# Softcapped attention ahead of two feed-forward layers: first keys loaded in two pieces, exps over three chunks, and the last keys' exps added to the sums by accumulating transfers

## The chip, the core and the metric

The kernel runs on one core of a Trainium2 chip. The core has a matmul engine (PE, with its weight loads shown apart as PEld), a vector engine (DVE), an activation engine (ACT), a general engine (POOL) and a queue engine that issues transfers (SP); POOL and ACT can issue transfers as well. Sixteen DMA engines move the data. Each engine works through its own list of instructions in order, and semaphores tie the lists together. The metric is the time of one execution in microseconds (us); lower is better.

## The reference

Attention over 2 batches and 12 heads with 448 positions and a head width of 64, then two feed-forward layers of 896 tokens, width 768 and inner width 2048. All in fp32.

```python
scores = scale * np.matmul(q, k.transpose(0, 1, 3, 2))
scores = cap * np.tanh(scores / cap)
attn = np.exp(scores - np.max(scores, axis=-1, keepdims=True))
attn = attn / (np.sum(attn, axis=-1, keepdims=True) + 1e-09)
x = np.matmul(attn, v)                    # heads side by side: 896 x 768
h = x @ w_in
x = (np.maximum(h, 0.0) + alpha * np.minimum(h, 0.0)) @ w_out
r = np.maximum(x @ w_in2, 0.0)
return (r * r) @ w_out2
```

## The kernel before

**Stages.** The attention takes about the first 97 us of the execution, the first feed-forward layer runs from there, the second after it. The feed-forward stages follow an order that a planner in the kernel worked out beforehand. The change doesn't touch the planner. The attention is written out by hand in `fast_attention`: six steps u = 0 to 5, and in each step four heads (two head pairs g = 0, 1, and two heads e = 0, 1 in a pair). The rows of PE, ACT and DVE stand in the order of the code. POOL and SP are ordered by the compiler from the same code.

**One step.** The 448 keys of a pair are cut in three full chunks of 128 keys and a rest of 64. So a step has seven chunks: 0 to 2 are the full chunks of pair 0, 3 to 5 those of pair 1, and chunk 6 holds both rests, pair 0 in partitions 0 to 63 and pair 1 in partitions 64 to 127. For every chunk PE multiplies keys with queries (`product`, lines 800 and 804) into one of three PSUM tiles `ps`, which are taken in turn; ACT takes the tanh of it into an SBUF tile `E` (line 819), which frees the PSUM tile, and later the exp in place (line 824). DVE adds up the exps over the chunks (`presum`): parts 1 and 2 add the chunks 0 to 2 to `s` of pair 0, parts 4 and 5 add the chunks 3 to 5 to `s` of pair 1 (line 840), and parts 6 and 7 add the two halves of chunk 6 to the two `s` (line 844, half of the partitions each). A step later PE multiplies the exps with the values (`values`, `last_values`, lines 852 and 862) and reduces the two `s` over the partitions with a matrix of ones (`sums`, line 871), which takes a `ps` tile too.

**A step's tail.** `evacuate` copies the sums (line 877, tile `rows`) and the two output tiles (line 883, `xu`) out of PSUM. Small transfers spread `rows` over partitions (line 880, tile `r`), `invert` takes 1/r on DVE and sends it on (lines 889 to 895, tile `rb`), and `normalise` multiplies `xu` with `rb` and splits the product in two parts for the next layer (lines 921 to 924). So step u runs the products, tanhs and exps of u, the values and sums of u - 1, the evacuation and the inverses of u - 2 and the normalisation of u - 3. Beside them `advance` prepares weights of the first feed-forward layer on DVE (lines 333 to 339, 938, 940).

**The end of the attention.** After step 5 PE runs three blocks of the first layer (`up_now`) among the rest: `up_now(0)`, the values and sums of step 5, `up_now(1)`, then `spread_last` (line 913), which needs the reciprocal of the last sums (line 903 on DVE, after line 902 on ACT), then `up_now(2)`.

**The start.** In `start`, SP issues the first keys and the first queries, one transfer each, while PE runs eight matmuls that only warm it up (line 766). Then PE multiplies the first 128 keys (line 771), and ACT starts on them.

Of the kernel before, what the change touches and what calls it, by code (L numbers as in the profile page):

```python
# [17 lines left out]
P = 128  # L18
# [6 lines left out]
FULL = 3  # L25
# [273 lines left out]
class Net:  # L299
# [443 lines left out]
    def start(self, ctx):  # L743
# [9 lines left out]

        first = self.raw[:, 1].bitcast(F32).rearrange("p n f -> p (n f)")
        k, q = (first[:, n * S:n * S + S] for n in range(2))
        nc.sync.dma_start(k, self.kT[:, 0])
        nc.sync.dma_start(q, self.qT[:, 0])
        self.kq = {0: (k, q)}
        self.ones = const.tile([P, P // 4], F32, name="ones")
        nc.gpsimd.memset(self.ones, 1.0)  # L760
# [46 lines left out]
    def tanh(self, u, *chunks):  # L807
        nc, S = self.nc, self.S
        es = self.es.setdefault(u, [])
        for n in chunks:  # L810
            if n % 2 == 0:
                shape = [P, min(2, 2 * FULL + 1 - n), 2, S]
                es.append(self.ap.tile(shape, F32, tag=f"E{shape[1]}", name="E", bufs=5 if shape[1] == 2 else 2))
            if u == n == 0:
                for e in range(2):
                    nc.scalar.activation(es[0][:, 0, e], self.outs[e], AF.Tanh, scale=self.scale_t)
                continue
            ps = self.early[n] if u == 0 and n in self.early else self.product(u, n)
            nc.scalar.activation(es[-1][:, n % 2], ps, AF.Tanh, scale=self.scale_t)  # L819

    def exp(self, u, m):

# [1 line left out]
        self.nc.scalar.activation(x, x, AF.Exp, scale=self.cap_t)  # L824

    def chunk(self, u, n):
        return self.es[u][n // 2][:, n % 2]

    def presum(self, u, *parts):

        nc, D, S = self.nc, self.D, self.S
        for part in parts:
            if part < 2 * FULL:
                g, c = divmod(part, FULL)
                if c == 0:
                    continue
                if c == 1:
                    self.ss[u, g] = self.ap.tile([P, 2, S], F32, tag="s", name="s", bufs=3)
                s = self.ss[u, g]
                nc.vector.tensor_add(s, self.chunk(u, part - 1) if c == 1 else s, self.chunk(u, part))  # L840
            else:
                rows = slice((part - 2 * FULL) * D, (part - 2 * FULL) * D + D)
                s = self.ss[u, part - 2 * FULL]
                nc.vector.tensor_add(s[rows], s[rows], self.chunk(u, 2 * FULL)[rows])

    def values(self, u, g):

# [94 lines left out]
    def fast_attention(self):  # L942
# [17 lines left out]
        for u in range(n):  # L960
            if u > 1:
                self.evacuate(u - 2)
            self.tanh(u, 0, 1, 2)
            self.exp(u, 0)
            if u:
                self.values(u - 1, 0)
                self.presum(u - 1, 4, 5, 6, 7)
                if u + 1 < n:
                    for g in range(2):
                        self.load_kq(2 * u + 2 + g)  # L970
            if u > 2:
                self.normalise(u - 3)
            self.tanh(u, 3, 4)
            self.exp(u, 1)
            self.presum(u, 1)
            if u > 1:
                self.invert(u - 2)
            if u:
                self.values(u - 1, 1)
                for m, steps in beside[u]:  # L980
                    self.advance(m, steps)
            self.tanh(u, 5, 6)
            if u < AHEAD - 1:
                self.fetch(u + 1)
            self.exp(u, 2)
            self.exp(u, 3)
            self.presum(u, 2)
            if u:
                self.last_values(u - 1)
                self.sums(u - 1)  # L990
                if u + 1 < n:
                    self.load_v(u + 1)
# [182 lines left out]
```

## Time and profile before

| | |
|---|---|
| runs of the kernel before | 521.12, 523.66, 524.09 us; median 523.66 |
| the profiled execution's own time | 522.88 us |
| its span in the profile | 520.8 us |
| busy in the span | PE 503.9 us (97%), DVE 469.2 (90%), ACT 395.0 (76%), POOL 36.9 (7%) |
| shares of the chain that ended last | PE 62%, DVE 15%, ACT 12%, DMA 5% |

How to read the rows further down: a row of the timeline is start, length, engine, line, operation, tile written `<-` tiles read, shape; `x2` merges two instructions in a row, and a bracket at the end says how long the engine had been idle before and for whom it waited. A row of the windows gives the stretch, its length and the busy time of each engine in it with the count of instructions, then the granted clock of PE, the mean busy share of the DMA engines and GB/s. The profiled execution's time of 522.88 us is its span plus 2.08 us around it.

### The profile page before, as it was taken

Reading aid. Unit: us, or ns where it says so; the run is one execution under the profiler, and the core shown is the slowest. Engines: PE = TensorE matmul, PEld = TensorE weight load, DVE = VectorE, ACT = ScalarE, POOL = GpSimd, SP = SyncE. Lnnn points to the kernel's source line nnn. Section 1 sums busy time; section 2 is a strip of 40 time slices with the busy share of each in tenths; the row PEclk is TensorE's granted clock in tenths of the full one; section 3 lists DMA queues with packets and bytes.
Section 4 is the critical chain, followed back from the end, with each engine's and each line's share of the span. In section 5 each row is a group of like instructions: output and inputs, shape, how many; then the busy total and the mean of one; then the engine's idle time right before and its main releaser. Section 6 shows DMA issues by size and latency. Waiting matters only on the chain.

```text
span 520.8 us, 6996 instructions
## 1 busy us (share of the span) xinstructions
PE 503.9 (97%) x2532; PEld 418.7 (80%) x2532; DVE 469.2 (90%) x698; ACT 395.0 (76%) x547; POOL 36.9 (7%) x51
## 2 busy tenths in 40 slices
PE   7899899999999999999999988999999999999996
PEld 2233234899999999999999977888989999999995
DVE  1689999899989999999979998899999999999961
ACT  6999994467687889755999947999677889946450
POOL 1000000000000000061500000100000002410000
PEclk9999999999999999999999999899999999999999
DMA  5744623156767565176835406566342229750011
GB/s 174 291 167 143 204 73 99 35 182 194 243 233 235 172 241 198 62 132 119 152 124 151 123 0 197 146 202 186 96 148 90 106 76 270 144 95 35 37 72 59
DMA packets 25195, 74.29 MB, mean 143 GB/s; under 512 B 4544, under 2 KB 15168, under 8 KB 25152
## 3 DMA queue, kind: packets, MB, share of 16 engines
q1 hardware_dynamic: 19392, 63.72, 37.4%
q0 software_dynamic: 5616, 10.03, 10.8%
q8 instruction: 22, 0.36, 0.3%
q14 instruction: 21, 0.17, 0.1%
q10 hardware_dynamic: 144, 0.00, 0.0%
HBM read 60.89 MB, written 2.79 MB: 122 GB/s over the span
## 4 chain that ended last, share of the span: by engine, by line
PE 62%; DVE 15%; ACT 12%; DMA 5%; issue 4%; SPq 1%; POOL 0%; DVEq 0%; ACTq 0%; POOLq 0%
PE hm L352 43%; PE out L352 14%; ACT raw L387 3%; DVE wl L434 2%; DMA r<-rows 2%; ACT wh L432 2%; ACT w L393 2%; DVE s L840 2%; DMA raw<-in_w 1%; ACT E L824 1%; ACT x L432 1%; ACT E L819 1%; PE ps L800 1%; DVE x L434 1%; PE out L852 1%
## 5 line engine op out<-in xcount | busy, mean ns | idle before, releaser
L352 PE MATMUL hm<-x,wh 128*128 128x448 f32 x916 | 258.1, 363 | 0.5 <-ACT g L509 0.4
L352 PEld LDWEIGHTS hm<-x,wh 128*128 128x128 f32 x916 | 171.7, 188 | 13.3 <-ACT g L509 1.6
L352 PE MATMUL hm<-x,wl 128*128 128x448 f32 x458 | 165.9, 362 | 0.0
L352 PEld LDWEIGHTS hm<-x,wl 128*128 128x128 f32 x458 | 86.0, 188 | 5.8
L352 PE MATMUL out<-x,wh 128*128 128x448 f32 x296 | 83.4, 362 | 0.2
L432 ACT CAST wh<-w 128x768 fp32r<-128x768 f32 x67 | 53.7, 805 | 22.0 <-PE hm L352 8.7
L432 ACT CAST x<-g 128x448 fp32r<-128x448 f32 x93 | 51.3, 571 | 22.3 <-DVE g L407 22.2
L387 ACT ACTIVATE raw<-raw 128x768 f16<-128x768 f32 x32 | 63.1, 1973 | 3.5 <-DVE raw L395 3.5
L434 DVE TENSOR_TENSOR wl<-w,wh 128x768 fp32r<-128x768 f32 x67 | 60.4, 902 | 1.1 <-ACT wh L432 0.9
L352 PEld LDWEIGHTS out<-x,wh 128*128 128x128 f32 x296 | 55.3, 187 | 4.6 <-ACT g L509 0.9
L434 DVE TENSOR_TENSOR x<-g,x 128x448 fp32r<-128x448 f32 x93 | 57.1, 616 | 0.6 <-ACT x L432 0.5
L352 PE MATMUL out<-x,wl 128*128 128x448 f32 x148 | 53.6, 362 | 0.0
L393 ACT ACTIVATE w<-raw 128x768 f32<-128x768 f32 x44 | 40.8, 931 | 11.4 <-DMA raw<-in_w 6.8
L391 DVE SCALAR_TENSOR_TENSOR w<-w,raw 128x768 int32<-128x768 int32 x44 | 41.8, 953 | 8.1 <-ACT raw L387 6.1
L819 ACT ACTIVATE E<-ps,scale_t 128x896 f32<-128x896 f32 x41 | 40.2, 1074 | 1.8 <-PE ps L800 1.8
L824 ACT ACTIVATE E<-E,cap_t 128x1792 f32<-128x1792 f32 (+1 forms) x24 | 38.9, 1667 | 0.0
L800 PE MATMUL ps<-q,k 64*128 64x448 f32 x132 | 30.4, 570 | 5.1 <-DVE rows L877 2.1
L407 DVE TENSOR_TENSOR g<-g,g 128x448 f32<-128x448 f32 x55 | 33.6, 616 | 1.1 <-ACT g L647 0.9
L352 PE MATMUL hm<-cx,wh 128*128 128x448 f32 x98 | 28.7, 375 | 3.1 <-ACT early L509 2.6
L432 ACT CAST wh<-cw 128x768 fp32r<-128x768 f32 x26 | 21.9, 844 | 12.7 <-DVE cw L407 6.5
L800 PEld LDWEIGHTS ps<-q,k 64*128 64x128 f32 x132 | 11.0, 185 | 24.5 <-ACT E L819 12.0
L852 PE MATMUL out<-E,v 128*64 128x448 f32 x144 | 29.5, 547 | 0.0
(141 smaller groups left out, 670.6 us busy)
## 6 DMA issues: line engine op xcount, KB each, us to landing
raw<-in_w SPq DMA_DIRECT2D x64, 768.0 KB, 4.2
x<-g POOLq DMA_DIRECT2D x12, 224.0 KB, 4.0
out_T<-g SPq DMA_DIRECT2D x12, 224.0 KB, 2.0
k<-in_kT SPq DMA_DIRECT2D x11, 224.0 KB, 4.8
q<-in_qT SPq DMA_DIRECT2D x11, 224.0 KB, 5.0
v<-in_vT SPq DMA_DIRECT2D x6, 384.0 KB, 4.8
rb<-row SPq DMA_DIRECT2D x10, 224.0 KB, 3.8
g<-g POOLq DMA_DIRECT2D x8, 224.0 KB, 5.2
```

What stands on the lines that cost most here:

```text
L352: self.nc.tensor.matmul(ps, a[:, c, :], m, start=first and n == 0 and not more, stop=last and n == 2, skip_group_check=more)
L387: nc.scalar.mul(halves[:, :, :, 1], parts()[1].bitcast(F32), sign * 2.0 ** -60)
L391: nc.vector.scalar_tensor_tensor(bits, bits, 3, parts()[0], op0=ALU.logical_shift_left, op1=ALU.bitwise_or)
L393: plan.op("ACT", self.act(n) + 0.06, lambda: nc.scalar.mul(w.tile, parts()[1].bitcast(F32), 2.0 ** -112), [high, raw], [w])
L407: plan.op("DVE", self.dve(n), lambda: getattr(nc.vector, op)(out.tile, a.tile, b.tile), [a, b], [out], port=True)
L432: plan.op("ACT", self.act(n), lambda: nc.scalar.mul(cut(h), w.tile, -1.0) if sign < 0 else nc.scalar.copy(cut(h), w.tile), reads, [h])
L434: if sign < 0 else nc.vector.tensor_sub(cut(l), w.tile, cut(h).bitcast(F32)), [*reads, h], [l], port=port)
L800: nc.tensor.matmul(ps[:, e, :], k[rows, c * P:c * P + P], q[rows], start=True, stop=True)
L819: nc.scalar.activation(es[-1][:, n % 2], ps, AF.Tanh, scale=self.scale_t)
L824: self.nc.scalar.activation(x, x, AF.Exp, scale=self.cap_t)
L840: nc.vector.tensor_add(s, self.chunk(u, part - 1) if c == 1 else s, self.chunk(u, part))
L852: nc.tensor.matmul(self.outs[g][rows], self.v[u][0][:, g, c, rows], self.chunk(u, g * FULL + c)[:, e], start=c == 0, stop=False)
```

## The change

Four edits, all in the attention. The first queries go out first on SP, the first 128 keys on ACT's queue behind the small transfer of `cap`, the other 320 keys on SP. The tiles `E` hold three chunks instead of two, four of them in turn instead of five, so that one exp covers three chunks: there are two long exps and a short one in a step where there were three and a short one. With that the rows of a step change places: tanh of chunks 3, 4, 5, then the exp of chunks 3 to 5, then tanh of chunk 6; PE runs the second half of `values` after product 5 and not before it; DVE runs parts 1 and 2 together. And in steps 0 to 4 the parts 6 and 7 are two transfers that POOL issues and that add in flight (224 KB each), where DVE had two additions; in step 5 DVE keeps them.

```diff
-        nc.sync.dma_start(k, self.kT[:, 0])
         nc.sync.dma_start(q, self.qT[:, 0])
+        nc.scalar.dma_start(k[:, :P], self.kT[:, 0, :P])
+        nc.sync.dma_start(k[:, P:], self.kT[:, 0, P:])
...
-            if n % 2 == 0:
-                shape = [P, min(2, 2 * FULL + 1 - n), 2, S]
-                es.append(self.ap.tile(shape, F32, tag=f"E{shape[1]}", name="E", bufs=5 if shape[1] == 2 else 2))
+            if n % FULL == 0:
+                shape = [P, min(FULL, 2 * FULL + 1 - n), 2, S]
+                es.append(self.ap.tile(shape, F32, tag=f"E{shape[1]}", name="E", bufs=4 if shape[1] == FULL else 2))
...
-                nc.vector.tensor_add(s[rows], s[rows], self.chunk(u, 2 * FULL)[rows])
+                x = self.chunk(u, 2 * FULL)[rows]
+                if u < self.NSTEP - 1:
+                    nc.gpsimd.dma_start(s[rows], x, accum_op=ALU.add)
+                else:
+                    nc.vector.tensor_add(s[rows], s[rows], x)
...
-            self.tanh(u, 3, 4)
-            self.exp(u, 1)
-            self.presum(u, 1)
+            self.tanh(u, 3, 4, 5)
+            self.presum(u, 1, 2)
             if u > 1:
                 self.invert(u - 2)
             if u:
                 self.values(u - 1, 1)
...
-            self.tanh(u, 5, 6)
+            self.exp(u, 1)
+            self.tanh(u, 6)
             if u < AHEAD - 1:
                 self.fetch(u + 1)
             self.exp(u, 2)
-            self.exp(u, 3)
-            self.presum(u, 2)
```

**ACT, from step 0 into step 1.** Before, from the tanh of chunk 1 of step 0 on (line 819 is a tanh of one chunk, 824 an exp; the number behind `ps` tells the three PSUM tiles apart):

```order
L819 ACTIVATE E<-ps_127,scale_t 128x896
L819 ACTIVATE E<-ps_128,scale_t 128x896
L824 ACTIVATE E<-E,cap_t 128x1792
L819 ACTIVATE E<-ps_129,scale_t 128x896
L819 ACTIVATE E<-ps_127,scale_t 128x896
L824 ACTIVATE E<-E,cap_t 128x1792
L819 ACTIVATE E<-ps_128,scale_t 128x896
L819 ACTIVATE E<-ps_129,scale_t 128x896
L824 ACTIVATE E<-E,cap_t 128x1792
L824 ACTIVATE E<-E,cap_t 128x896
L819 ACTIVATE E<-ps_127,scale_t 128x896
```

The same place now:

```order
L820 ACTIVATE E<-ps_128,scale_t 128x896
L820 ACTIVATE E<-ps_129,scale_t 128x896
L825 ACTIVATE E<-E,cap_t 128x2688
L820 ACTIVATE E<-ps_130,scale_t 128x896
L820 ACTIVATE E<-ps_128,scale_t 128x896
L820 ACTIVATE E<-ps_129,scale_t 128x896
L825 ACTIVATE E<-E,cap_t 128x2688
L820 ACTIVATE E<-ps_130,scale_t 128x896
L825 ACTIVATE E<-E,cap_t 128x896
L820 ACTIVATE E<-ps_128,scale_t 128x896
```

The tanh of chunk 6, the last line 819 (820) row before step 1, had two exps of two chunks ahead of it and one behind; now it has two exps of three chunks ahead of it.

**DVE, in step 3.** Before, from the copy of the sums of step 1 to the inverse of step 1:

```order
L877 COPY rows<-ps_127 128x448
L883 COPY xu<-out_85 128x448
L883 COPY xu<-out_86 128x448
L840 TENSOR_TENSOR s<-E 128x896
L840 TENSOR_TENSOR s<-s,E 128x896
L844 TENSOR_TENSOR s<-s,E 64x896 x2
L921 TENSOR_TENSOR xs<-xu,rb 128x896
L923 CAST x<-xs 128x896
L924 TENSOR_TENSOR x<-xs,x 128x896
L840 TENSOR_TENSOR s<-E 128x896
L889 TENSOR_SCALAR r<-r,guard_t 128x14
```

The same place now:

```order
L882 COPY rows<-ps_128 128x448
L888 COPY xu<-out_86 128x448
L888 COPY xu<-out_87 128x448
L841 TENSOR_TENSOR s<-E 128x896
L841 TENSOR_TENSOR s<-s,E 128x896
L926 TENSOR_TENSOR xs<-xu,rb 128x896
L928 CAST x<-xs 128x896
L929 TENSOR_TENSOR x<-xs,x 128x896
L841 TENSOR_TENSOR s<-E 128x896
L841 TENSOR_TENSOR s<-s,E 128x896
L894 TENSOR_SCALAR r<-r,guard_t 128x14
```

The two additions of line 844 are gone, and the second addition for pair 0, which stood at the end of the step behind the weight preparation, stands ahead of the inverse.

**POOL, in the attention.** Before, the end of its setup and the first transfers that it issues, which belong to the feed-forward layers:

```order
L949 MEMSET choice 128x256
L953 MEMSET choice 1x64 x4
L788 ISA
L788 TENSOR_SCALAR minus_t<-slope_t 128x16
L417 DMA w_785<-cw 128x768
```

The same place now:

```order
L954 MEMSET choice 128x256
L958 MEMSET choice 1x64 x4
L789 ISA
L789 TENSOR_SCALAR minus_t<-slope_t 128x16
L847 DMA s<-E 64x896 x10
L417 DMA w_774<-cw 128x768
```

Ten transfers of chunk 6 to `s`, two for each of steps 0 to 4, stand on a queue that had nothing to do in the attention. PE's line 871 (now 876) waits for them, pair 0 for the first, pair 1 for the second.

## Rows read from the trace of the kernel before

**Rows 1.** The page's busy times: engine, us, share of the span, instructions.
```profile
PE 503.9 (97%) x2532; PEld 418.7 (80%) x2532; DVE 469.2 (90%) x698; ACT 395.0 (76%) x547; POOL 36.9 (7%) x51
```

**Rows 2.** Waits of PE in the first 110 us: waiting, releaser, total us, times, longest.
```profile
PE ps L800 <- DVE rows L877: 2.1, 2, 1.6
...
PE ps L913 <- DVE rows L903: 0.6, 1, 0.6
```

**Rows 3.** Windows by PE's steps 2 to 5, and the first feed-forward stage.
```profile
27.67:40.29 12.62, 12.62 (x72) 4.18 (x72) 11.28 (x16) 12.62 (x12) 0.00 (x0) 1.00 0.51 173
40.29:52.77 12.48, 12.48 (x76) 4.28 (x73) 11.88 (x16) 12.48 (x13) 0.00 (x0) 1.00 0.49 150
52.77:67.17 14.40, 12.75 (x77) 4.20 (x73) 14.06 (x20) 13.24 (x13) 0.00 (x0) 1.00 0.55 184
67.17:80.41 13.24, 12.75 (x77) 4.19 (x73) 13.00 (x17) 12.55 (x12) 0.00 (x0) 1.00 0.26 72
...
96.36:251.00 154.64, 154.64 (x774) 144.72 (x773) 148.78 (x214) 111.81 (x173) 13.21 (x15) 1.00 0.58 172
```

**Rows 4.** Timeline of DVE in step 3 and into step 4.
```profile
42.47 1.09 DVE L840 TENSOR_TENSOR s<-E 128x896 f32<-128x896 f32 x1 [0.30 <-ACT E L824]
...
44.60 2.20 DVE L844 TENSOR_TENSOR s<-s,E 64x896 f32<-64x896 f32 x2
...
48.03 0.63 DVE L923 CAST x<-xs 128x896 fp32r<-128x896 f32 x1
...
55.52 0.61 DVE L877 COPY rows<-ps 128x448 f32<-128x448 f32 x1
```

**Rows 5.** Timeline of ACT at the end of step 0.
```profile
12.65 1.82 ACT L824 ACTIVATE E<-E,cap_t 128x1792 f32<-128x1792 f32 x1
14.33 1.93 ACT L819 ACTIVATE E<-ps,scale_t 128x896 f32<-128x896 f32 x2
16.11 2.76 ACT L824 ACTIVATE E<-E,cap_t 128x1792 f32<-128x1792 f32 x2
18.72 2.84 ACT L819 ACTIVATE E<-ps,scale_t 128x896 f32<-128x896 f32 x3
```

**Rows 6.** Timeline of PE: products of chunks 1 and 2 of step 1.
```profile
15.42 1.92 PE L800 MATMUL ps<-q,k 64*128 64x448 f32 x8 [1.54 <-ACT E L819]
```

**Rows 7.** Timeline of the end: ACT, DVE and PE around the last sums.
```profile
90.82 0.64 ACT L902 ACTIVATE rows<-ps,guard_t 128x448 f32<-128x448 f32 x1 [5.51 <-DMA row<-r]
...
91.02 1.09 DVE L924 TENSOR_TENSOR x<-xs,x 128x896 fp32r<-128x896 f32 x1
...
92.03 2.94 DVE L903 RECIPROCAL rows<-rows 128x448 f32<-128x448 f32 x1
...
95.12 1.74 PE L913 MATMUL ps<-rows,choice 128*128 128x448 f32 x4 [0.56 <-DVE rows L903]
```

**Rows 8.** Timeline of PE: the sums of step 2, in step 3.
```profile
51.88 0.96 PE L871 MATMUL ps<-s,ones 128*32 128x448 f32 x8
```

**Rows 9.** One line's instructions: POOL's issues (ns), landings of lines 417, 426, 895.
```profile
L417 POOL DMA_DIRECT2D g<-g x8: 859/862/1062, 225.9 to 245.6; - x8
...
DMA to landing us min/median/max: 3.1/5.4/7.7
...
DMA to landing us min/median/max: 3.0/4.0/8.3
...
DMA to landing us min/median/max: 3.4/3.8/4.9
```

**Rows 10.** Timeline of PE at the start, and landing of the first keys and queries.
```profile
1.48 3.59 PE L766 MATMUL warm<-x 128*128 128x512 bf16 x8 [1.48 <-POOL x L762]
5.13 1.15 PE L771 MATMUL out<-raw 64*128 64x448 f32 x4
...
DMA to landing us min/median/max: 3.2/3.3/3.3
```

More of the change, by code (lines that the diff above doesn't have):

```diff
@@ L818, in tanh @@
             ps = self.early[n] if u == 0 and n in self.early else self.product(u, n)
-            nc.scalar.activation(es[-1][:, n % 2], ps, AF.Tanh, scale=self.scale_t)
+            nc.scalar.activation(es[-1][:, n % FULL], ps, AF.Tanh, scale=self.scale_t)
     def exp(self, u, m):
@@ L826, in chunk @@
     def chunk(self, u, n):
-        return self.es[u][n // 2][:, n % 2]
+        return self.es[u][n // FULL][:, n % FULL]
     def presum(self, u, *parts):
```

## The prediction, as made before the changed kernel ran

> **What bounds the kernel now.** I read the page's busy times first: PE is busy for 97% of the span [rows 1], so a change off PE can only give back the time in which PE waits. From 96.36 us to 251 us PE is busy for the whole of 154.64 us [rows 3], so an earlier end of the attention moves the rest forward, one for one, and nothing in that stage can swallow it before 251 us. What matters is thus when PE leaves the attention.
>
> There I listed PE's waits. Two are for DVE's copy of the sums, 2.1 us together, and one of 0.6 us is for DVE's last reciprocal [rows 2]. The windows cut at PE's steps show where: steps 2 and 3 take 12.62 and 12.48 us with PE busy all the time, step 4 takes 14.40 and step 5 13.24 [rows 3]. In step 4 DVE is busy for 14.06 of 14.40 us, so there DVE sets the pace; in steps 2 and 3 it has room and PE sets it, with ACT just as full (12.62 of 12.62). The clock is 1.00 throughout. So three engines stand within two microseconds of each other, and taking work off one of them uncovers the next.
>
> **The change, part by part.**
>
> *Parts 6 and 7 off DVE.* Each of steps 1 to 5 loses two additions of 2.20 us together, standing from 44.60 us on in step 3 [rows 4]: 11.0 us of DVE in all. How much of that PE sees is bounded by its own step. At PE's mean pace of (12.62 + 12.48)/2 = 12.55 us, steps 4 and 5 would shrink by 14.40 + 13.24 - 2 x 12.55 = **2.54 us**. Is DVE really out of the way then? In step 3 it runs from the first addition at 42.47 us to the copy at 55.52 us without a real gap, 13.05 us; without the 2.20 that is 10.85. That addition starts some 1.9 us into a step (a copy and two more precede it), so DVE comes to the next copy 12.75 us into a step of 12.55: 0.2 us late, against the 1.75 us that PE needs for two products (about 0.88 each, 1.92 for two with the drain [rows 6]) before it wants that PSUM tile. It fits, with about 0.9 us to spare once the copy's own 0.61 us is counted. Where this slack is gone (say the small transfers of 1/r land later behind the new ones), step 4 alone loses what exceeds it; I take nothing, with 1 us as the other bound.
>
> *Exps over three chunks.* On ACT a tanh follows the last after 0.89 us (1.78 for two), an exp of two chunks takes 1.68 (12.65 to 14.33), an exp of two and one of one together 2.61, so one chunk 0.93 [rows 5]. A chunk more costs 1.68 - 0.93 = 0.75, so an exp of three is put at 2.45 (2.43 by this step, 2.47 by the tanh's share: no matter). A step's ACT work goes from 7 x 0.89 + 3 x 1.68 + 0.93 = 12.20 to 7 x 0.89 + 2 x 2.45 + 0.93 = 12.06 us. Under PE's 12.55 this brings nothing. The Trainium skill, page "ScalarE: Activation LUTs", section "What ACT_TABLE_LOAD costs", lets an ACTIVATE with pointer operands carry a fixed part of which about 0.09 us overlaps with its neighbour, so a merged one would save some 0.19 us by an estimate from that page; the rows give 0.1, and by either the sum stays, since PE covers it.
>
> *The tanh of chunk 6 comes later.* This is the cost I find in the diff. The three PSUM tiles go round, and in step 1, the first with nothing summed before it, product 2 takes the tile that the tanh of chunk 6 of step 0 frees. Before, that tanh starts at 14.33 + 0.89 = 15.22 us and PE's products 1 and 2, which had been waiting for ACT for 1.54 us already, run through from 15.42 us [rows 5, 6]. Now two exps of three stand ahead of it: step 0's first exp starts where it did, at 12.65 - 1.78 - 1.68 = 9.19 us, and then 2.45 + 3 x 0.89 + 2.45 put the tanh at 16.76 us, **1.54 us later**. Behind product 2 PE's list is full (values, products, sums), so step 2 begins 1.54 us later than 27.67 us, at 29.2. In later steps product 1 takes the tile of chunk 6. With a step's first tanh about 1.1 us after PE's first product (0.88 and the drain), the tanh of chunk 6 ends 1.1 + 6 x 0.89 + 2 x 2.45 + 1.04 = 12.4 us into the step, and PE wants the tile at 12.55 + 0.88 = 13.4. So this is paid once. Bounds: 0 if the PE list had slack before step 2 that I don't see, 1.54 if not; I take 1.54, because the window of step 2 shows PE without a gap [rows 3].
>
> *Parts 6 and 7 as transfers.* They leave when DVE has done part 5, at 44.60 us in step 3, and PE's sums start at 51.88 us [rows 4, 8]: a margin of 7.28 us, and the moved DVE rows don't shorten it. POOL needs 0.86 us to issue one, and those that add in flight land 3.0 to 8.3 us after the start of their issue, medians 5.4 and 4.0 (lines 417 and 426); a transfer of this very shape to 64 partitions, though without the addition (line 895), takes 3.4 to 4.9 [rows 9]. The first of the two leaves earlier, as soon as the last exp is done. I take 5.4 us, which fits, and price 0; the other bound is the slowest, 8.3 us, which overruns by 1.0 us in each of five steps, 5.1 us.
>
> *First keys and queries.* The warm-up matmuls end at 1.48 + 3.59 = 5.07 us and the first product starts at 5.13; the transfers take 3.2 and 3.3 us from issue [rows 10] and are issued by 1.2 us, so they are there by 4.5. The edit can bring at most the 0.06 us between, and I take 0. The cover is the warm-up; without it some 0.5 us would show. On ACT one more issue stands ahead of work that has 2 us to spare.
>
> *The end.* ACT delivers the last sums at 90.82 + 0.64 = 91.46 us, but DVE is busy with line 924 and starts the reciprocal only at 92.03; PE waits 0.56 us for it [rows 7]. DVE enters the end without its backlog, 1.5 us or more earlier, so the reciprocal starts when ACT is done and PE's wait goes: **0.55 us**. Step 5 keeps its own two additions, so nothing else moves here.
>
> **Sum.** 2.54 - 1.54 + 0.55 = 1.55 us less than the profiled execution's 522.88 us (span 520.8 and 2.08 around it): 521.3 us. That execution lies 0.78 us under the median of the runs, so against the median of 523.66 I expect **522.1 us**.
>
> **Rivals.**
>
> *A, the sum above:* 522.1 us; 520.6 to 523.7 with the bounds of step 4 (1 us) and the spread of the runs.
>
> *B, the late tanh costs nothing,* because PE has hidden slack in step 1: then the whole of 2.54 + 0.55 = 3.1 us comes through, 520.6 us. For it speaks that ACT, not PE, is what step 1 waits for; against it that PE is seen busy from there on without a gap [rows 3]. This is also the most that the change can give, as PE has no other waits on DVE.
>
> *C, slower: the transfers that add land after PE wants them.* Place: PE's sums at the end of steps 1 to 5, with the next step's products queued behind them, and ACT behind those. Price: what the landing exceeds 7.28 us, five times. At 8.3 us it is 5.1 us, and 523.66 - 1.55 + 5.1 = 527.2 us. It eats the gain at 7.28 + 1.55/5 = 7.6 us and makes the kernel slower by 1% at about 8.65. For it: landings up to 7.7 and 8.3 us do occur, DMA engines are already busy for half of the time in steps 2 to 4, and two such transfers meet the loads of the next step. Against it: both medians leave two microseconds. A mechanism that could cause it is DVE holding POOL's descriptors back; each of DVE's short copies (0.63 us, [rows 4]) would add its length, 5.4 + 0.63 = 6.0, still inside the margin, and held back for the whole rest of DVE's run (8.7 us) it would make five times 6.8 us, 556 us. The trace speaks against the strong form: the landings of 3.0 to 7.7 us of line 417 include the stretch in which DVE was busy for 148.78 of 154.64 us [rows 3, 9]. The Trainium skill, page "SBUF — State Buffer", section "SBUF: two separate sides", states this lock: while DVE runs an operation that takes both ports, descriptors for a transfer issued from POOL can't be written.
>
> *D, no effect:* DVE stays late for another reason (its inverse waits for the small transfers, which now share the DMA engines), and what steps 4 and 5 give goes in step 1: 523.7 us.
>
> **Chances.** A 0.57, B 0.15, C 0.18 (the strong form of the lock 0.02 of it), D 0.10. A measurement of this kernel tells about 1%, 5.2 us, from no change. Faster than 518.4 us none of the cases gives; 0.04 is left for what I don't see. Slower than 528.9 us takes C with landings beyond 8.65 us: 0.07. Within 1%: 0.89. The range holds A, B and the nearer half of C, with the 3 us over which the runs of the kernel before spread: 519.4 to 525.5 us; the far half of C and a run below 519.4 are left out, 0.2 together.
>
> **What would show it.** In the changed kernel: no wait of PE for line 882 (rows) and steps 4 and 5 at 12.5 us each; step 2 beginning near 29.2 us instead of 27.67, with a wait of PE for a tanh ahead of product 2 of step 1; step 5 ending near 79.4 us instead of 80.41; line 908 starting right after ACT's line 907; landings of line 847 under 7 us and no wait of PE at line 876. Wrong would be: a wait at line 876 for `s` (C), step 2 at 27.7 us (B), or waits for line 882 still there (D).

## The result, and the profile after

The changed kernel takes 528.04 us (median of 4 runs, 526.83 to 529.29), the kernel before beside it 523.52 us (521.12 to 524.09). The ratio is 1.0097, with an interval of 1.0076 to 1.0118: about 4.5 us slower, outside the predicted range of 519.4 to 525.5 us. The attention lost what it was to gain.

The page's busy times of the changed kernel, and its windows by PE's steps 2 to 5, for [rows 1, 3]:

```profile
PE 504.9 (96%) x2532; PEld 418.8 (80%) x2532; DVE 458.9 (87%) x688; ACT 395.3 (75%) x541; POOL 46.8 (9%) x61
```

```profile
29.58:42.83 13.25, 12.55 (x76) 4.28 (x73) 7.20 (x11) 13.15 (x12) 1.62 (x2) 1.00 0.72 198
42.83:58.09 15.26, 13.70 (x77) 4.36 (x73) 11.32 (x17) 14.46 (x13) 1.62 (x3) 1.00 0.57 152
58.09:73.00 14.91, 12.55 (x75) 4.29 (x73) 12.72 (x18) 11.52 (x9) 2.01 (x2) 1.00 0.77 210
73.00:86.08 13.08, 12.55 (x77) 4.28 (x73) 10.37 (x14) 12.58 (x11) 1.62 (x2) 1.00 0.54 106
```

DVE is busy for 10.3 us less, about the work that the diff takes from it. Yet the four steps take 56.50 us instead of 52.74. In step 2 ACT is nearly full (13.15 of 13.25 us), and PE waits 0.70 us for a tanh. In steps 3 to 5 no engine is full: DVE is busy for 12.72 of 14.91 us at most, ACT for 14.46 of 15.26, and PE stands idle for 0.53 to 2.36 us in each. What they wait for, by the waits of PE and DVE in the first 110 us, for [rows 2]:

```profile
PE ps L801 <- DVE rows L882: 4.0, 3, 2.4
PE ps L876 <- DMA s<-E: 0.5, 1, 0.5
```

```profile
DVE r L894 <- DMA r<-rows: 6.5, 3, 2.5
DVE xs L926 <- DMA rb<-row: 4.9, 3, 2.5
```

DVE's 6.5 us for `r` are new; before, DVE had no listed wait for `r` and 1.5 us for `rb`. PE's sums wait once for an adding transfer. The listed 0.5 us are only a part of what that took, by PE's timeline in step 3:

```profile
55.78 0.94 PE L876 MATMUL ps<-s,ones 128*32 128x448 f32 x4
57.21 0.95 PE L876 MATMUL ps<-s,ones 128*32 128x448 f32 x4 [0.48 <-DMA s<-E]
```

The sums went on until 58.09 us, 2.31 us for what takes 0.89 in step 4 (72.11 to 73.00): 1.4 us lost, once. The timeline of DVE around step 3's end shows how a late `r` becomes a wait of PE:

```profile
54.51 1.09 DVE L841 TENSOR_TENSOR s<-s,E 128x896 f32<-128x896 f32 x1
57.73 0.23 DVE L894 TENSOR_SCALAR r<-r,guard_t 128x14 f32<-128x14 f32 x1 [2.14 <-DMA r<-rows]
58.00 0.24 DVE L895 RECIPROCAL r<-r 128x14 f32<-128x14 f32 x1
...
60.68 0.96 DVE L945 TENSOR_TENSOR wl<-ww,wh 128x768 fp32r<-128x768 f32 x1
61.55 0.61 DVE L882 COPY rows<-ps 128x448 f32<-128x448 f32 x1
```

DVE's list is in order: behind the inverse, which ends at 58.24 us, stand 3.3 us of weight preparation, and behind that the copy `rows` that gives PE its PSUM tile back. PE had begun step 4 at 58.09 us and wanted that tile two products later; the copy started at 61.55.

Why `r` is late stands in SP's own timeline. In step 2, first of the kernel before, then of the changed one:

```profile
30.89 2.79 SPq L880 DMA_DIRECT2D r<-rows  x4
```

```profile
31.37 0.38 SPq L730 DMA_DIRECT2D k<-in_kT  x1
...
33.45 0.38 SPq L740 DMA_DIRECT2D vt<-in_vt  x1
33.92 3.63 SPq L885 DMA_DIRECT2D r<-rows  x4
```

The four transfers of `r` are 1.8 KB each, but SP issues them behind the next step's loads (four of k and q, 224 KB each, v of 384 and vt of 64, and in steps 2 and 4 a weight block of 768). In the changed kernel DVE's copy of the sums ended at 30.98 us, and `r` went out from 33.92 us on, 2.94 us later (1.93 before). The issue of one `r` lasted up to 1.97 us, where 0.61 was the most before; why isn't shown. The chain that ended last has the last `r` of this step landing 5.25 us after its issue (start, length, what):

```profile
37.05 5.25 DMA r<-rows
```

The transfers of 27 to 92 us tell what became of the loads: first the kernel before, then the changed one (issues, KB each, median us to landing).

```profile
k<-in_kT SPq DMA_DIRECT2D x6, 224.0 KB, 4.9
r<-rows SPq DMA_DIRECT2D x20, 1.8 KB, 3.8
vt<-in_vt SPq DMA_DIRECT2D x4, 64.0 KB, 4.9
```

```profile
s<-E POOLq DMA_DIRECT2D x8, 224.0 KB, 5.2
k<-in_kT SPq DMA_DIRECT2D x6, 224.0 KB, 6.4
r<-rows SPq DMA_DIRECT2D x20, 1.8 KB, 4.3
vt<-in_vt SPq DMA_DIRECT2D x4, 64.0 KB, 6.5
```

So **theory 1**: the adding transfers share the DMA engines with the loads; the loads take 1.5 us longer; `r`, queued behind them, comes late; DVE and then PE wait. (PE itself hardly waits for the loads: 0.3 us for q, 1.3 before.) **Theory 2**: the place of `r` doesn't matter, the transfers just take long. **Theory 3**: the new dependency, the adding itself, is the price. The three-chunk exps and the first loads are tried apart.

The place of the loss, by the timeline of PE. The first tanh comes 0.72 us later (7.08 for 6.36), which is scatter, as shown further down. From it to step 2 go 22.50 us instead of 21.31 (+1.19). Steps 2 to 5 take +3.76. PE's last wait, for the reciprocal, is 1.20 us for 0.56 [rows 7]. Together 6.3 us, and they stay until about 320 us. At the border of the two layers 2.4 come back in these two profiles: there the kernel before waited for 2.59 us (the changed one 1.58) and then ran at a lower clock. The windows there (the column behind POOL is the granted clock), before and after:

```profile
326.00:330.00 4.00, 3.58 (x10) 3.22 (x11) 4.00 (x7) 4.00 (x5) 0.86 (x1) 0.57 0.77 201
```

```profile
332.00:336.00 4.00, 4.00 (x21) 3.75 (x21) 4.00 (x8) 4.00 (x5) 0.41 (x1) 1.00 0.96 238
```

### The profile page after: what moved, and what is told of

The parts are those of the page before. It is cut to its first block, busy times and chain, and to the rows that moved or that the text cites. A ratio compares the mean times of both kernels' runs of the same rounds, so it can differ in the third digit from the quotient of the medians.

```text
span 524.9 us, 7028 instructions
## 1 busy us (share of the span) xinstructions
PE 504.9 (96%) x2532; PEld 418.8 (80%) x2532; DVE 458.9 (87%) x688; ACT 395.3 (75%) x541; POOL 46.8 (9%) x61
## 4 chain that ended last, share of the span: by engine, by line
PE 58%; DVE 15%; ACT 12%; DMA 10%; issue 3%; SPq 1%; POOL 0%; DVEq 0%; ACTq 0%; POOLq 0%
PE hm L352 42%; PE out L352 14%; ACT raw L387 3%; DMA v<-in_vT 2%; DVE wl L434 2%; DMA raw<-in_w 2%; DMA r<-rows 2%; ACT E L825 2%; ACT w L393 2%; ACT E L820 1%; ACT wh L432 1%; DVE w L391 1%; DMA k<-in_kT 1%; DVE x L434 1%; ACT x L432 1%
## 5 line engine op out<-in xcount | busy, mean ns | idle before, releaser
L820 ACT ACTIVATE E<-ps,scale_t 128x896 f32<-128x896 f32 x41 | 38.9, 998 | 4.4 <-PE ps L801 4.4
L825 ACT ACTIVATE E<-E,cap_t 128x2688 f32<-128x2688 f32 (+1 forms) x18 | 36.7, 2039 | 0.6
L841 DVE TENSOR_TENSOR s<-E 128x896 f32<-128x896 f32 x12 | 13.0, 1084 | 19.1 <-ACT E L825 19.1
```

The costliest lines, as they stand in the source:

```text
L820: nc.scalar.activation(es[-1][:, n % FULL], ps, AF.Tanh, scale=self.scale_t)
```

## Experiments: the edits apart

Each was timed beside the kernel before, whose medians there were 522.64 to 523.0 us. "First tanh to step 2" is 21.30 to 21.31 us in each kernel with exps over two chunks, the kernel before included.

**The accumulating transfers alone**, on the kernel before:

```diff
-                nc.vector.tensor_add(s[rows], s[rows], self.chunk(u, 2 * FULL)[rows])
+                x = self.chunk(u, 2 * FULL)[rows]
+                if u < self.NSTEP - 1:
+                    nc.gpsimd.dma_start(s[rows], x, accum_op=ALU.add)
+                else:
+                    nc.vector.tensor_add(s[rows], s[rows], x)
```

> The kernel before with one edit alone: parts 6 and 7 of steps 0 to 4 are the accumulating transfers; exps over two chunks, their order and the first loads as before. Theory 1 (the transfers are what hurts: they share the DMA engines with the small transfers of 1/r, which land later, and DVE waits for them): steps 2 to 5, 52.7 us before and 56.5 after, take 55 us or more, DVE waits over 3 us for r and rb, and the time is 2 to 4 us over the kernel before. Rival 2 (the late exps and the moved order of DVE hurt, the transfers alone help): DVE loses its backlog, PE's waits for the copy of the sums (2.1 us) go, steps 2 to 5 take 50 to 51.5 us and the time is 1 to 2.5 us under the kernel before.

Measured: 528.85 us, ratio 1.0112 (1.0083 to 1.0141): theory 1 in kind, and 6.2 us where it gave 2 to 4. Steps 2 to 5 take 61.62 us. Some 3.3 us of that is PE at a lower clock behind its waits: the granted clock is 0.90 in the mean of steps 4 and 5, and PE is busy for 14.45 and 14.39 us there, not 12.75. The waits of DVE and PE:

```profile
DVE r L893 <- DMA r<-rows: 12.0, 3, 6.5
```

```profile
PE ps L800 <- DVE rows L881: 7.4, 3, 3.1
```

**All but the transfers** (DVE adds in every step):

> The changed kernel with parts 6 and 7 back on DVE in every step; exps over three chunks and the first loads in two pieces stay. Theory 1 (the transfers hurt): r and rb land as before, but DVE has its 2.2 us a step back; steps 2 to 5 take 52 to 54 us, step 2 still begins near 29.6 us, and the time is 1 to 3 us over the kernel before. Rival 2 (the order hurts): 56 us or more for steps 2 to 5, time 4 us or more over the kernel before.

Measured: 524.88 us, 1.005 (1.0034 to 1.0066). This lies in theory 1's range. DVE doesn't wait for `r`, but step 2 begins 24.19 us after the first tanh, at 31.12 us and not near 29.6.

**The first loads alone:**

> The kernel before with the first loads alone changed (queries first, the first 128 keys on ACT's queue, the rest behind). If these loads brought the late start (the first products 0.7 us late in the changed kernel, at half the clock): the first tanh starts at 7.1 us instead of 6.4 and the time is 0.5 to 1 us over the kernel before. If the late start is a matter of when the clock is granted, and not of the edit: within 0.5 us of the kernel before, with the first tanh at 6.4 or at 7.1 us independent of the edit.

Measured: 522.62 us, 1.0007 (0.9988 to 1.0027). The edit does nothing. Its first tanh comes at 7.08 us, as in the changed kernel; but the other kernels with the same edit show 5.98 to 7.02, and one without it (the last of the experiments) shows 7.08 too, so that is scatter from run to run.

**The changed kernel without the first loads:**

> The changed kernel with the first loads as before. If the edit of the loads costs the 0.7 us of the start: 0.5 to 1 us faster than the changed kernel, so 3.5 to 4 us over the kernel before. If not: 4.5 us over it, like the changed kernel. By both, the exps over three chunks leave PE idle for about 2 us before product 6 of step 0, and step 2 begins at 29 us or later.

Measured: 527.97 us, 1.0122 (1.0088 to 1.0157). The same as the changed kernel.

**The three-chunk exps alone**, on the kernel before:

```diff
-            self.tanh(u, 3, 4)
-            self.exp(u, 1)
-            self.presum(u, 1)
+            self.tanh(u, 3, 4, 5)
+            self.presum(u, 1, 2)
...
-            self.tanh(u, 5, 6)
+            self.exp(u, 1)
+            self.tanh(u, 6)
...
-            self.exp(u, 3)
-            self.presum(u, 2)
```

> The kernel before with the three-chunk exps alone: old first loads, additions on VectorE. Theory 1 (each edit pays apart): as the changed kernel with additions on VectorE, 524.0 to 525.5 us, step 2 begins 2 to 3 us later than before's 27.7, and steps 2 to 5 together take no longer than before's 52.7. Rival (the loss needs the later first products): 522 to 523.5 us.

Measured: 524.99 us, 1.004 (1.0026 to 1.0054), as theory 1 had it. So the transfers cost about 1%, the exps 0.4%, the first loads nothing. The timeline of PE in step 1 of this kernel, for [rows 6], and the granted clock beside it:

```profile
14.11 1.91 PE L800 MATMUL ps<-q,k 64*128 64x448 f32 x8
18.45 1.02 PE L800 MATMUL ps<-q,k 64*128 64x448 f32 x4 [2.44 <-ACT E L819]
19.41 4.17 PE L852 MATMUL out<-E,v 128*64 128x448 f32 x12
```

```profile
20.00:23.00 3.00, 3.00 (x12) 0.82 (x8) 1.84 (x2) 2.97 (x4) 0.00 (x0) 0.50 0.77 309
```

Product 2 waits for the late tanh as predicted. Then PE runs at the lower of its two levels (0.50 is 1.2 GHz): twelve matmuls take 4.17 us that take 2.48 elsewhere, 1.69 us lost where PE is full. In the changed kernel product 2 starts as late (11.73 us after the first tanh in both), but the low clock fell ahead of it, on time in which PE would have waited for this tanh: the wait there is 0.93 us, not 2.44. So the changed kernel shows what the tanh alone costs, 1.19 us (22.50 us), and 1.69 more makes the 2.9 us by which step 2 comes later here (24.20 us).

## Experiments: why the transfers cost

**Plain copies as traffic.** DVE still adds; POOL copies the same data to a tile that nobody reads:

```diff
+                if u < self.NSTEP - 1:
+                    nc.gpsimd.dma_start(self.spare[rows], x)
                 nc.vector.tensor_add(s[rows], s[rows], x)
```

> The kernel before, VectorE still making its two additions, and beside them GpSimd copies the same halves of chunk 6 (224 to 256 KB in steps 0 to 4) to a tile that nobody reads; this adds work that the output does not need. Theory 1 (it is the traffic on the shared DMA engines that makes r late): waits of VectorE for r appear that the kernel before has not, and the time is 2 to 6 us over before, 525 to 529 us. Theory 3 (it is the new dependency: PE's sums wait for the accumulating transfers, or the adding itself): the time stays within 1 us of before.

Measured: 525.36 us, 1.0057 (1.0035 to 1.0078). This lies in theory 1's range and not in theory 3's. DVE's waits name `r`, though no engine reads what the new transfers write:

```profile
DVE r L892 <- DMA r<-rows: 4.4, 3, 1.8
```

So traffic alone makes `r` late, and theory 3 isn't needed for it. But plain copies cost about half of what the adding ones do (0.6% against 1.1%), though the loads beside them land as late (k in 6.4 us, and 6.5 beside the adding ones alone). The queues show a difference: the software queue, which holds POOL's transfers, from 27 to 92 us, with its share of the 16 DMA engines' time, for plain copies and for adding ones alone.

```profile
q0 software_dynamic: 384, 1.84, 10.8%
```

```profile
q0 software_dynamic: 640, 1.84, 16.9%
```

The same 1.84 MB take 10.8% of the engines' time as copies and 16.9% when they add (19.4% in the changed kernel). That the dearer transfers cost more by this is likely, but no run tests it.

**SP in the order of the code.** In all kernels above the compiler orders SP. Here the changed kernel's SP keeps the order in which the code is written, so `r` goes out ahead of the next k and q:

```diff
-                    engines = {mybir.EngineType.PE, mybir.EngineType.Activation, mybir.EngineType.DVE}
+                    engines = {mybir.EngineType.PE, mybir.EngineType.Activation, mybir.EngineType.DVE, mybir.EngineType.SP}
```

> The changed kernel with SyncE's transfers issued in the order of the code, so that the four small transfers of the reciprocal (r) go out ahead of the next step's k, q and vt loads instead of behind them. Theory 1 (the accumulating transfers slow the loads, and r pays because it lands behind them in SP's order): DVE's wait for r, 6.5 us in three in the changed kernel, falls to about 0; steps 2 to 5 take 50 to 53 us instead of 56.5, and the time is 2 to 4 us under the changed kernel's 528.0, 524 to 526 us. Theory 2 (the place of r in the queue does not matter; DVE and PE wait because the transfers themselves take long): the wait moves to another transfer, and the time stays at 527 us or more.

Measured: 519.21 us, 0.9929 (0.9904 to 0.9953): 8.8 us under the changed kernel and faster than before, more than either theory gave. The wait for `r` and the steps:

```profile
DVE r L894 <- DMA r<-rows: 0.7, 1, 0.7
```

```profile
30.12:42.40 12.28, 12.28 (x76) 4.37 (x72) 8.80 (x13) 12.18 (x11) 1.61 (x2) 1.00 0.59 124
...
54.68:66.95 12.27, 12.27 (x76) 4.36 (x72) 11.57 (x16) 12.17 (x11) 2.01 (x2) 1.00 0.80 190
66.95:79.31 12.36, 12.36 (x77) 4.29 (x73) 10.96 (x15) 12.26 (x11) 2.07 (x2) 1.00 0.62 115
```

PE is busy in every step from end to end, though the DMA engines are about as busy as in the changed kernel (up to 0.80 here, 0.77 there). Steps 2 to 5 take 49.19 us; step 4, bound by DVE before [rows 3], has 12.27. Theory 2, with 527 us or more, falls. SP's timeline in step 2, where DVE's copy of the sums ends at 30.98 us again:

```profile
31.01 3.56 SPq L885 DMA_DIRECT2D r<-rows  x4
34.62 0.58 SPq L730 DMA_DIRECT2D k<-in_kT  x1
```

`r` leaves at once and not 2.94 us later. The edit moves the loads too, though, and beside the same adding transfers they now land sooner (k in 3.9 us, not 6.4), so this run alone doesn't tell `r`'s place from theirs.

**Is it the order alone?** The same line on the kernel before, and on the three-chunk kernel with DVE's additions:

> The kernel before with SyncE's transfers in the order of the code, and nothing else. Theory 1 (in the kernel before VectorE's own work holds up steps 4 and 5, r is on time there; the order of the queue matters only beside the accumulating transfers): steps 4 and 5 still take over 13 us, and the time lies within 1.5 us of before, 521.5 to 523.5 us. Rival (the gain of the changed kernel with this order, 519.2 us, comes from the order alone): 519 to 520.5 us, steps 4 and 5 below 12.8 us each.

Measured: 521.54 us, 0.9978 (0.9965 to 0.9992). Steps 4 and 5 still take 14.40 and 13.17 us, as theory 1 had it. There is a small gain, which the steps don't show; I haven't found it (the profiled execution took 522.81 us and may not have it).

> The changed kernel with the additions on VectorE in all steps, and SyncE's transfers in the order of the code. Theory 1 (taking the additions from VectorE is what gives steps 4 and 5 their 12.3 us, once r comes early): steps 4 and 5 take over 13 us here, and the time is 523 to 525 us, as the 524.9 of the same kernel with the old order. Rival (the order alone gives the gain): 519 to 520.5 us.

Measured: 524.03 us, 1.004 (1.0018 to 1.0062); steps 4 and 5 take 14.18 and 13.32 us: theory 1 again. Neither has the gain: it takes the additions off DVE *and* SP in the order of the code.

**Transfers and order, exps over two chunks:**

> The kernel before with the accumulating transfers alone (528.9 us) and SyncE's transfers in the order of the code; exps over two chunks and first loads as before. Theory 1 (r's place behind the loads is what the transfers' cost hangs on, and the three-chunk exps cost their late tanh in step 0 apart): VectorE's wait for r falls from 12 us to under 2, step 2 begins at 27.5 to 28.5 us, steps 2 to 5 take 49.5 to 51.5 us, and the time is 517.5 to 519.5 us, at or under the 519.2 of the changed kernel with this order. Rival (the three-chunk exps are needed for it, since ScalarE with one exp more is the bound then): steps 2 to 5 at 51.5 us or more, 520 us or more.

Measured: 517.67 us, 0.9904 (0.987 to 0.9938), the fastest of all and what theory 1 gave. Its windows:

```profile
27.61:40.23 12.62, 12.62 (x72) 4.19 (x72) 9.24 (x14) 12.62 (x12) 1.61 (x2) 1.00 0.48 115
...
52.71:65.20 12.49, 12.49 (x76) 4.19 (x72) 10.20 (x15) 12.49 (x13) 1.61 (x2) 1.00 0.76 177
65.20:78.42 13.22, 12.76 (x77) 4.20 (x73) 10.45 (x15) 12.84 (x12) 1.61 (x2) 1.00 0.53 114
```

The transfers cost 1.1% in the compiler's order. In the code's order they bring 0.7%: 517.67 us against 521.54 for the kernel before with that order, timed beside each other. In step 5 PE waits 0.46 us for `rows`; why that copy is late is open. DVE's wait for `rb` is 4.3 us in this fastest kernel (4.9 in the changed one), so that wait isn't the price.

**`r` alone on another queue**: the changed kernel, SP's other transfers as they were:

```diff
-            nc.sync.dma_start(r[n:n + P // 4], rows[n:n + 1])
+            nc.gpsimd.dma_start(r[n:n + P // 4], rows[n:n + 1])
```

> The changed kernel as it is, SyncE's order too, but the four small transfers of r are issued by GpSimd on its queue instead of SyncE's. Theory 1 (what costs is r's place behind the loads in SyncE's order): VectorE's wait for r falls from 6.5 us to under 2.5, steps 2 to 5 take 49 to 52 us instead of 56.5, and the time is 519 to 524 us. Rival (the loads themselves, or the later row and rb transfers, must move too): 526 us or more.

Measured: 523.61 us, 1.002 (0.9996 to 1.0043): 4.4 us under the changed kernel. Steps 2 to 5 take 52.52 us, and

```profile
DVE r L894 <- DMA r<-rows: 3.4, 2, 2.0
```

The time is in theory 1's range, the steps are just over it, and half of the wait is left (2.5 or less was expected). Only `r` moved here, and the loads land no sooner than in the changed kernel (k in 7.9 us), so `r`'s place is worth about half of the 8.8 us. Where the other half lies isn't shown; the loads' own place is one candidate. Another is that `r` now stands behind an adding transfer in POOL's list (issued at 31.92 us in step 2, `r` from 32.44 on). The Trainium skill, page "DMA: Bandwidth & Descriptors", section "Rules for kernel authors", says that spreading transfers over issuing engines gives no bandwidth, as all share 16 engines, and saves only the time of issuing. The runs agree: `r` took longer to land than from SP (median 5.8 us, 4.3 in the changed kernel), but in step 2 it left 1.0 us after DVE's copy and not 2.94. For a short transfer that something waits for, that did matter: 6.5 us of waiting against 3.4.

## Experiments: what the three-chunk exps lose

**Step 0 with its tanhs first**: tanhs 0 to 3, an exp, tanhs 4 to 6, two exps, in step 0 alone, without the adding transfers; then the same with transfers and SP in the code's order.

```diff
-            self.tanh(u, 0, 1, 2)
+            self.tanh(u, *((0, 1, 2) if u else (0, 1, 2, 3)))
...
-            self.tanh(u, 3, 4, 5)
+            self.tanh(u, *((3, 4, 5) if u else (4, 5, 6)))
...
-            self.tanh(u, 6)
+            if u:
+                self.tanh(u, 6)
```

> The three-chunk exps and the first loads of the changed kernel with the additions on VectorE in all steps, and in step 0 alone ScalarE's order changed: tanhs 0 to 3, the first exp, tanhs 4 to 6, the second and third exp. Theory 1 (what the three-chunk exps lose is the late tanh of chunk 6 of step 0 and PE's idle time there, with the stretch of half granted clock behind it): step 2 begins at 27.7 to 28.7 us instead of 31.1, the half-clock stretch near 14 to 24 us is gone, and the time is 1.5 to 2.5 us under the 524.9 of the same kernel with the old order, 522.4 to 523.4 us. Rival (the loss lies elsewhere or is given back later): 524.4 us or more.

Measured: 524.56 us, 1.0037 (1.0018 to 1.0056), by time the rival's case. Step 2 begins in time, 21.28 us after the first tanh, with no stretch of low clock there. But the wait came back one step later, again for a tanh of chunk 6 (PE's timeline):

```profile
28.30 1.02 PE L801 MATMUL ps<-q,k 64*128 64x448 f32 x4
31.00 1.77 PE L801 MATMUL ps<-q,k 64*128 64x448 f32 x8 [1.68 <-ACT E L820]
```

> The changed kernel with SyncE's transfers in the order of the code, and in step 0 ScalarE's order tanhs 0 to 3, first exp, tanhs 4 to 6, second and third exp. Theory 1 (the late tanh and the half-clock stretch behind it cost 1.5 to 2 us; what step 2 lost in the trial with VectorE's additions was VectorE's lateness, which is gone here): step 2 begins at 27.7 to 28.7 us, steps 2 to 5 take 49 to 50 us, 517.3 to 518.5 us. Rival (step 2 takes 14 us again, since the sums of step 0 are then late for another reason): 518.8 us or more.

Measured: 518.76 us, 0.992 (0.9896 to 0.9945), no more than scatter under the 519.21 without it and between the two theories. Step 2 takes 14.10 us here (14.23 without the transfers), and the low clock is back, from 15 to 18 us. Theory 1 was half right in both: the stall is a backlog of ACT, and one step's order only moves it.

**The order of step 0 in every step.** ACT's step is longer than I had priced. By its timeline in the kernel with SP in the code's order:

```profile
31.22 2.80 ACT L820 ACTIVATE E<-ps,scale_t 128x896 f32<-128x896 f32 x3
34.06 2.53 ACT L825 ACTIVATE E<-E,cap_t 128x2688 f32<-128x2688 f32 x1
36.50 2.78 ACT L820 ACTIVATE E<-ps,scale_t 128x896 f32<-128x896 f32 x3
```

An exp of three takes 2.44 us (36.50 - 34.06), as put. But it starts 2.84 us behind its three tanhs, where 3 x 0.89 is 2.67: an exp directly behind the tanh that fills its tile starts some 0.15 us late. Three such places make ACT's step 12.5 us (31.22 to 43.73), not 12.06. That is more than PE's own 12.28: here ACT falls back by 0.2 us in every step, and with the tanhs of step 0 first as well, steps 3 to 5 take ACT's 12.48 us. With the tanh of chunk 3 ahead of the first exp and that of chunk 6 ahead of the second this goes:

```diff
-            self.tanh(u, 0, 1, 2)
+            self.tanh(u, 0, 1, 2, 3)
...
-            self.tanh(u, 3, 4, 5)
+            self.tanh(u, 4, 5, 6)
...
-            self.tanh(u, 6)
```

> The kernel before with three-chunk exps, additions on VectorE and old first loads, and in every step ScalarE's order tanhs 0 to 3, first exp, tanhs 4 to 6, second exp, third exp: no exp comes directly behind the tanh that fills the last part of its tile, but for the second. Theory 1 (an exp directly behind its own tanh waits some 0.15 us for it, three times in a step, so ScalarE's step takes 12.5 us; this and the late tanh of chunk 6 are the loss of 2 us): exps start 0.89 to 0.93 us behind the tanh ahead of them but for the second, ScalarE's step takes 12.2 us or less, step 2 begins by 28.2 us and takes under 12.8, and the time is 522 to 523.2 us, 1.5 to 3 under the 525.0 of the same kernel with the old order. Rival (VectorE's later additions and later sums are the loss): 524.2 us or more.

Measured: 526.56 us, 1.0072 (1.0042 to 1.0101), worse and in the rival's range. ACT's rows are as expected (four tanhs, and the exp 3.56 = 4 x 0.89 us behind the first):

```profile
19.31 3.71 ACT L819 ACTIVATE E<-ps,scale_t 128x896 f32<-128x896 f32 x4
22.87 2.58 ACT L824 ACTIVATE E<-E,cap_t 128x2688 f32<-128x2688 f32 x1
```

But PE waits for tanhs twice in steps 0 and 1 (2.01 and 1.83 us) and step 2 begins 26.20 us after the first tanh. So ACT's 0.15 us are real, and they aren't the loss; theory 1 fell here. The rival's reason isn't shown either: steps 2 to 5 take 52.40 us, about as with the three-chunk exps alone (52.11). The loss lies ahead of step 2, where PE waits for tanhs while the engines fill, and there the clock falls twice (to 0.50 near 15 to 18 and 22 to 25 us).

> The order of late on top of the accumulating transfers and SyncE's transfers in the order of the code. Theory 1: steps 2 to 5 take 12.3 to 12.6 us each, step 2 begins by 28.2 us, and the time is 515.5 to 517.7 us, at or under the 517.7 of the same kernel with exps over two chunks. Rival: the exps in one stretch at the end of the step make the accumulating transfers, which then leave 1 us or more into the next step, late for the sums: waits of PE for s, 518.5 us or more.

Measured: 523.34 us, 1.0008 (0.9987 to 1.0028), with runs from 520.84 to 525.63. Steps 2 to 5 take 12.43 to 12.44 us each and no wait of PE for `s` is listed; step 2 begins 23.46 us after the first tanh. The steps are as theory 1 had them, the time isn't, and the rival's reason doesn't show either; the one profiled execution, with a span of 518.7 us the fastest of the ten, doesn't explain the spread.

## Why the prediction was wrong, step by step

*The step that failed* is the last of "Parts 6 and 7 off DVE": that the small transfers of 1/r might land later was bounded at 1 us, in step 4 alone, and taken as nothing. Measured, DVE waits 6.5 us for `r`, in three steps, and steps 2 to 5 take 56.50 us, not the 50.2 of the sum (4 x 12.55). With the order of SP's queue changed and nothing else they take 49.19. Of the 7.4 us over PE's own pace (4 x 12.28), 1.0 is the late tanh in step 2 (13.25 - 12.28) and 1.4 the late `s` in step 3; the other 5.0 stand where PE waits for the copies `rows` behind a late `r`. I had priced the new transfers only against their own consumer and left out what they do to other transfers on the same engines, and to the short ones that stand last.

*Rival D had the mechanism* ("its inverse waits for the small transfers, which now share the DMA engines"), but as a case without effect, at 523.7 us and 0.10. It was written as keeping DVE's old lateness; in fact DVE came later than before.

*Rival C had a small part of it.* Landings were 4.2 to 7.9 us, median 5.2, inside the bounds drawn from [rows 9] (where line 417 begins at 3.1 us and not at the 3.0 that the text repeats). PE's sums lost 1.4 us, in one step and not in five. The margin of 7.28 us didn't hold there: DVE was late, so the second transfer of step 3 left at 49.56 us, 6.73 us into the step where the sum had 4.31. Its time of 527.2 us came near mostly for another reason.

*Parts 6 and 7, the gain of 2.54 us:* right once `r` is early. Steps 4 and 5 shrink from 27.64 us to 24.63 in the changed kernel with SP in code order, 3.0 us, as PE's three-chunk step is 12.28 us and not 12.55. With exps over two chunks they take 25.71 us (12.49 + 13.22), 1.9 us less than before.

*Exps over three chunks:* an exp of three at 2.44 us was right, ACT's step of 12.06 us was not (12.5). That is more than PE's 12.28, so merging the exps made ACT the slower of the two; over the few steps here the backlog stayed small.

*The late tanh:* right in place and kind; step 2 begins at 29.58 us against the predicted 29.2, of which 0.72 is the later start, so the tanh cost 1.19 us and not 1.54. Two errors nearly cancel: the tanh of chunk 6 starts 10.69 us after the first tanh, 1.83 later than before, since both exps ahead of it start late by the 0.15 us; and from the values behind product 2 PE needs 9.82 us to step 2 where it needed 10.40, slack that the sum put at nothing. What the sum lacked is the lower clock behind PE's waits, 1.7 us where it falls on a full PE and nothing in the changed kernel's profile. "Paid once" was wrong: in step 2 of the changed kernel PE waits 0.70 us for a tanh again, and with step 0 mended 1.68.

*First keys and queries:* zero was right (1.0007).

*The end:* -0.55 us was wrong for the changed kernel (+0.64), since DVE entered the end with its backlog. ACT delivered at 97.13 us, DVE was busy with line 929 until 98.34:

```profile
97.33 1.09 DVE L929 TENSOR_TENSOR x<-xs,x 128x896 fp32r<-128x896 f32 x1
98.34 2.95 DVE L908 RECIPROCAL rows<-rows 128x448 f32<-128x448 f32 x1
```

With SP in the code's order the changed kernel has no listed wait of PE there, as the prediction had it; with exps over two chunks and that order it is 1.1 us.

## What to carry to other kernels

When work moves from an engine to a transfer, ask not only when the new transfer lands but which transfers already there get slower, and which short one with a waiting engine stands behind them in its queue; issue that short one first. Read the same change with the queue's order both ways: here the same transfers are 1.1% worse or 0.7% better by that alone. A merged instruction saves its overhead but makes its consumers wait for the last part; look where the pipeline fills, before the steady state.

## What the runs showed of the hardware

- An adding transfer took more of the DMA engines' time than a copy of the same bytes: 16.9 to 22.5% in the kernels that have them alone on POOL's queue, against 10.8% as plain copies, for 1.84 MB between 27 and 92 us.
- PE's clock fell to the 1.2 GHz level for some 3 us soon after waits of PE: in the changed kernel behind one of 2.06 us (0.50 from 14 to 17 us), with the three-chunk exps alone behind two of 1.52 and 2.44 us. It happened ahead of 25 us in ten of the eleven profiled kernels with three-chunk exps and in none of the six with two chunks. The six waited for tanhs there too, for 1.53 or 1.54 us and once more for 1.1 us at most. The eleventh, with step 0's tanhs first and DVE's additions, waited for 2.01 and 0.82 us there and kept its clock; the same order with the transfers also waited for 2.01 us and lost it. So I can't say from these rows what decides. With the transfers alone the clock fell after the waits for `rows`, to a mean of 0.90 in each of steps 4 and 5.
- The start of ACT's first tanh varies by itself: 5.88 to 7.08 us after the start of the span over these profiles, without an edit that accounts for it.
- ACT's exp directly behind the tanh that fills its tile started some 0.15 us later than one with another tanh between: 2.84 us behind the start of three tanhs, where 3 x 0.89 is 2.67, and 3.56, 4 x 0.89, behind four of which the last fills another tile.
